# Decode attention: P as the stationary operand of PV, and an identity that stays loaded

## Chip, cores, metric

One core of one Trainium2 chip. The metric is the device time of one execution, in microseconds. The kernel before takes 1312.33 us (median of three runs, 1312.21 to 1312.5).

## The reference, cut

One decoded token, 32 heads of width 128, each with its own cache of 32,768 keys and values, in parallel with a SwiGLU block on the same normalised input. All inputs are bf16.

```python
xn = layernorm(x)                                        # (1, 1, 640)
q  = (xn @ wq).reshape(1, 1, 32, 128)
s  = einsum("bhqd,bhkd->bhqk", q, k_cache) * 128 ** -0.5  # 32768 scores per head
o  = einsum("bhqk,bhkd->bhqd", softmax(s), v_cache)
out = x + o.reshape(1, 1, 4096) @ wo + (silu(xn @ w_gate) * (xn @ w_up)) @ w_down
```

K and V are 537 MB of the 554 MB that have to be read. Nothing of them is used twice.

## The kernel before, the parts that matter

Keys lie as 128 partitions times 256. A unit of load is a chunk of 128 keys a partition: 4 MiB, 32 KiB a partition. A ring of six such slots holds K and V chunks by turns; the sync engine issues every load, in order, each as soon as its slot is free. VectorE multiplies K by q in place, TensorE (PE) adds up the 128 products of a key in 16 groups of eight, with an identity as the stationary operand, and VectorE sums the eight that are left. ScalarE makes P from the scores of a head. PV goes one key column at a time.

```python
units = [("wq",), ("ffn",)]
for h in range(H):
    for c in range(NCH):                      # NCH = 2 chunks a head
        units.append(("k", h, c))
        if h >= 1:
            units.append(("v", h - 1, c))
units += [("wo",)]
units += [("v", H - 1, c) for c in range(NCH)]
# ... slots by position modulo 6 ...

def scores(k):                                # TensorE, 2 halves a chunk
    ...
    for g in range(DH // G):                  # 16 matmuls of 512 columns a half
        mm = t.matmul(ob, lhsT=ident[:, :], rhs=kv[:, i * HF:(i + 1) * HF, g * G:(g + 1) * G],
                      start=(g == 0), stop=(g == DH // G - 1))
    mm.then_inc(s_qk, 1)                      # frees the K slot after the second half

def pv_ops(h, c):                             # TensorE, 128 times a chunk
    ...
    mm = t.matmul(O[h % 2], lhsT=ring[:, s, j * DH:(j + 1) * DH],     # V: 128 x 128, stationary
                  rhs=P[:, h % PR, jj:jj + 1], start=(jj == 0), stop=(jj == NJ - 1))
    ...
    mm.then_inc(s_pv, 1)                      # frees the V slot

# sync engine: a V load waits until PV of the chunk that lay there is done
e.dma_start(ring[:, s, :], kv_src(A_v_cache, h, c * CH, CH)).then_inc(s_slot[s], 16)
```

Every matmul here is two instructions in the program, a weight load and the matmul. The kernel is fully unrolled: 22,786 instructions in the trace, 21,692 of them weight loads and matmuls.

## Time and profile before

| | before |
|---|---|
| median time, us | 1312.33 |
| TensorE matmul busy / weight load busy / VectorE busy, us | 852.6 / 492.8 / 682.5 |
| mean granted TensorE clock | 0.731 |
| loads of K, V, weights: MB, share of 16 DMA engines' span | 554.0, 98.8% |
| instruction fetch (queue 8): packets, MB, share | 85, 1.39, 0.4% |

In the profile's lines PE stands for TensorE's matmuls, PEld for its weight loads, DVE for VectorE, ACT for ScalarE, POOL for GpSimd, SPq for the sync engine that issues the loads; L235 is line 235 of that run's kernel, and x is a count. From the page of the kernel before: the busy line of the engines, then three rows of 40 slices of the span (the clock in tenths, the DMA engines' busy share in tenths, the rate), and two of the DMA queues (packets, MB, share of 16 engines' span).

```profile
span 1310.3 us, 22786 instructions
...
PE 852.6 (65%) x10846; PEld 492.8 (38%) x10846; DVE 682.5 (52%) x405; ACT 31.6 (2%) x108; POOL 1.1 (0%) x8
...
PEclk9677776776776766776776776776776766776775
DMA  9999999999999999999999999999999999999987
GB/s 394 431 430 429 430 431 429 430 430 431 431 431 430 429 429 431 430 430 430 429 431 430 430 431 430 429 432 431 430 429 429 430 431 431 430 431 430 430 352 295
...
q1 hardware_dynamic: 23920, 554.00, 98.8%
q8 instruction: 85, 1.39, 0.4%
```

The reader is to see a DMA row of nines, and 429 to 432 GB/s from the second to the 38th slice, while TensorE's clock goes up and down between 0.6 and 0.8. So the stream of loads is the limit and the engines follow it. The two last slices are lower: there lie the loads of wo, in packets of 1,280 bytes, and the end. And there is a small queue 8, of the kind "instruction", with 1.39 MB and 0.4% of the 16 DMA engines' time: in this table the instructions themselves come over the DMA engines too.

Groups of instructions and DMA issues of the page of before (count, busy us, mean ns of one, idle before; for the issues, KB each and median us from issue to landing):

```profile
L235 PE MATMUL ps<-ring,ident 128*128 128x512 bf16 x2048 | 585.8, 457 | 417.9 <-DVE ring L439 417.9
...
L257 PEld LDWEIGHTS ps<-P,ring 128*128 128x128 bf16 x8192 | 219.1, 97 | 20.4 <-issue 10.5
L257 PE MATMUL ps<-P,ring 128*128 128x1 bf16 x8192 | 221.3, 163 | 5.7 <-DMA ring<-in_A_v_cache_dram 5.2
...
ring<-in_A_k_cache_dram SPq DMA_DIRECT2D x64, 4096.0 KB, 45.1
ring<-in_A_v_cache_dram SPq DMA_DIRECT2D x63, 4096.0 KB, 51.5
```

A K load takes 45.1 us from issue to landing where 4 MiB at 430 GB/s are 9.75 us: about 35 us of loads are always queued ahead of it. The sync engine's own waits for slots (us in total, times, longest):

```profile
SPq L174 <- PE ps L235: 934.8, 60, 18.8
SPq L184 <- PE ps L257: 184.4, 59, 3.3
```

Timeline of before near 617 us (start, duration, engine, line, operation, count), one score chunk and the PV after it:

```profile
617.16 0.13 PEld L235 LDWEIGHTS ps<-ring,ident 128*128 128x128 bf16 x2 [6.76 <-DVE ring L439]
...
619.28 0.15 PEld L235 LDWEIGHTS ps<-ring,ident 128*128 128x128 bf16 x1 [0.28 <-issue]
619.71 0.15 PEld L235 LDWEIGHTS ps<-ring,ident 128*128 128x128 bf16 x1 [0.28 <-issue]
...
626.42 3.44 PEld L257 LDWEIGHTS ps<-P,ring 128*128 128x128 bf16 x128
626.53 3.41 PE L257 MATMUL ps<-P,ring 128*128 128x1 bf16 x128
```

In the first stretch the weight loads, and so the matmuls, are 427 ns apart (619.28 to 619.71, clock 0.5). PV of a whole V chunk, 128 weight loads and 128 matmuls, is done in 3.4 us.

### The profile page before, as it was taken

What the parts mean: (1) busy time and instruction counts of PE and PEld (TensorE: products, weight loads), DVE (VectorE), ACT (ScalarE), POOL (GpSimd) and SP (SyncE); (2) the same over time, 40 slices, a digit from 0 to 9 for tenths busy, and PEclk for the clock granted to TensorE, in tenths of its full rate; (3) what the DMA queues carried; (4) which work ended last, traced back from release to release, by engine and by line L of the source; (5) the groups of instructions that cost most, each with busy time, mean ns of one, the idle gap of its engine ahead of it and who ended that gap; (6) DMA issues with size and microseconds to landing.
All of it is one profiled execution on the core that took longest, in us unless ns stands there. A gap on an engine that the chain in (4) does not pass through costs nothing.

```text
span 1310.3 us, 22786 instructions
## 1 busy us (share of the span) xinstructions
PE 852.6 (65%) x10846; PEld 492.8 (38%) x10846; DVE 682.5 (52%) x405; ACT 31.6 (2%) x108; POOL 1.1 (0%) x8
## 2 busy tenths in 40 slices
PE   3777675675675676675675675675675676675675
PEld 1534342343343333342433342333433333343434
DVE  0566456455456455456455456455456455456450
ACT  2000000000000000000000000000000000000000
POOL 0000000000000000000000000000000000000000
PEclk9677776776776766776776776776776766776775
DMA  9999999999999999999999999999999999999987
GB/s 394 431 430 429 430 431 429 430 430 431 431 431 430 429 429 431 430 430 430 429 431 430 430 431 430 429 432 431 430 429 429 430 431 431 430 431 430 430 352 295
DMA packets 24011, 555.45 MB, mean 424 GB/s; under 512 B 2480, under 2 KB 6640, under 8 KB 6896
## 3 DMA queue, kind: packets, MB, share of 16 engines
q1 hardware_dynamic: 23920, 554.00, 98.8%
q8 instruction: 85, 1.39, 0.4%
q14 instruction: 6, 0.05, 0.0%
HBM read 553.99 MB, written 0.00 MB: 423 GB/s over the span
## 4 chain that ended last, share of the span: by engine, by line
DMA 73%; PE 17%; DVE 8%; SPq 1%; issue 0%; DVEq 0%
DMA ring<-in_A_k_cache_dram 71%; PE ps L235 17%; DVE ring L439 8%; DMA ring<-in_A_v_cache_dram 2%; SPq L184 0%; SPq L179 0%; SPq L189 0%; DVE sc L447 0%; PE ps L257 0%; SPq L191 0%; DVEq L435 0%; SPq L188 0%; DVE pmax L454 0%; SPq L187 0%; SPq L170 0%
## 5 line engine op out<-in xcount | busy, mean ns | idle before, releaser
L235 PE MATMUL ps<-ring,ident 128*128 128x512 bf16 x2048 | 585.8, 457 | 417.9 <-DVE ring L439 417.9
L439 DVE TENSOR_TENSOR ring<-ring,qb 128x8192 bf16<-128x8192 bf16 x128 | 560.7, 4422 | 206.4 <-DMA ring<-in_A_k_cache_dram 206.4
L235 PEld LDWEIGHTS ps<-ring,ident 128*128 128x128 bf16 x2048 | 228.6, 114 | 749.4 <-DVE ring L439 423.6
L447 DVE TENSOR_REDUCE sc<-ps 128x64 f32<-128x512 f32 x128 | 88.5, 692 | 270.1 <-PE ps L235 270.1
L257 PEld LDWEIGHTS ps<-P,ring 128*128 128x128 bf16 x8192 | 219.1, 97 | 20.4 <-issue 10.5
L257 PE MATMUL ps<-P,ring 128*128 128x1 bf16 x8192 | 221.3, 163 | 5.7 <-DMA ring<-in_A_v_cache_dram 5.2
L368 ACT ACTIVATE P<-sc,negb 128x256 bf16<-128x256 f32 x32 | 16.2, 507 | 1214.6 <-DVE negb L462 1214.6
L462 DVE TENSOR_SCALAR negb<-ps 128x1 f32<-128x1 f32 x32 | 5.1, 158 | 56.8 <-PE ps L286 56.8
L457 DVE TENSOR_REDUCE m<-ps 1x1 f32<-1x128 f32 x32 | 8.9, 279 | 23.6 <-PE ps L280 23.6
L219 PE MATMUL ps<-ring,xnb 128*128 128x512 bf16 x40 | 11.0, 444 | 11.7 <-DMA ring<-in_A_wq_dram 11.7
L411 DVE TENSOR_SCALAR sg<-sg 128x13 f32<-128x13 f32 (+1 forms) x2 | 0.2, 157 | 34.9 <-ACT sg L351 34.9
L286 PE MATMUL ps<-m,ones 1*128 1x1 f32 x64 | 14.5, 293 | 0.4 <-DVE m L457 0.4
L454 DVE TENSOR_REDUCE pmax<-sc 128x1 f32<-128x256 f32 x32 | 13.4, 420 | 1.1
L274 PEld LDWEIGHTS ps<-rsum,ones 128*128 128x128 f32 x64 | 12.3, 194 | 4.5
L280 PE MATMUL ps<-identf,pmax 128*1 128x128 f32 x64 | 12.1, 271 | 1.2 <-DVE pmax L454 1.2
L286 PEld LDWEIGHTS ps<-m,ones 1*128 1x128 f32 x64 | 11.8, 228 | 1.2 <-DVE m L457 0.7
L427 DVE RECIPROCAL rzb<-ps 128x1 f32<-128x1 f32 x32 | 5.1, 158 | 13.6 <-PE ps L274 13.6
L295 PE MATMUL ps<-xn,ring 128*128 128x1 bf16 (+1 forms) x140 | 8.7, 198 | 5.0 <-DMA ring<-in_B_w_down_dram 5.0
L311 PE MATMUL ps<-ocol,ring 128*128 128x1 bf16 x160 | 6.7, 178 | 7.3 <-DMA ring<-in_A_wo_dram 6.9
L219 PEld LDWEIGHTS ps<-ring,xnb 128*128 128x128 bf16 x40 | 4.3, 110 | 17.9 <-issue 14.8
L295 PEld LDWEIGHTS ps<-xn,ring 128*128 128x128 bf16 (+1 forms) x140 | 8.6, 161 | 5.5 <-issue 5.4
L311 PEld LDWEIGHTS ps<-ocol,ring 128*128 128x128 bf16 x160 | 6.6, 131 | 7.4 <-DMA ring<-in_A_wo_dram 7.0
(40 smaller groups left out, 46.5 us busy)
## 6 DMA issues: line engine op xcount, KB each, us to landing
ring<-in_A_k_cache_dram SPq DMA_DIRECT2D x64, 4096.0 KB, 45.1
ring<-in_A_v_cache_dram SPq DMA_DIRECT2D x63, 4096.0 KB, 51.5
ring<-in_A_wq_dram SPq DMA_DIRECT2D x1, 5120.0 KB, 15.3
ring<-in_A_wo_dram SPq DMA_DIRECT2D x1, 5120.0 KB, 45.3
ring<-in_B_w_gate_dram SPq DMA_DIRECT2D x1, 2160.0 KB, 20.0
ring<-in_B_w_up_dram SPq DMA_DIRECT2D x1, 2160.0 KB, 24.7
ring<-in_B_w_down_dram SPq DMA_DIRECT2D x1, 2080.0 KB, 28.6
ring<-in_A_v_cache_dram SPq DMA_DIRECT2D x1, 2048.0 KB, 21.3
```

The lines of the kernel that those rows point to most:

```text
L219: mm = t.matmul(bank[b], lhsT=xnb[:, c, :], rhs=wq_v[:, c, b * 512:(b + 1) * 512], start=(c == 0), stop=(c == NCD - 1))
L235: mm = t.matmul(ob, lhsT=ident[:, :], rhs=kv[:, i * HF:(i + 1) * HF, g * G:(g + 1) * G], start=(g == 0), stop=(g == DH // G - 1))
L257: mm = t.matmul(O[h % 2], lhsT=ring[:, s, j * DH:(j + 1) * DH], rhs=P[:, h % PR, jj:jj + 1], start=(jj == 0), stop=(jj == NJ - 1))
L274: t.matmul(misc[:, 129:130], lhsT=ones[:, :], rhs=rsum[:, h % SR:h % SR + 1], start=True, stop=True).then_inc(s_z, 1)
L280: t.matmul(misc[0:1, 0:128], lhsT=pmax[:, h % SR:h % SR + 1], rhs=identf[:, :], start=True, stop=True).then_inc(s_t, 1)
L286: t.matmul(misc[:, 128:129], lhsT=ones[0:1, :], rhs=m1[0:1, h % SR:h % SR + 1], start=True, stop=True).then_inc(s_b, 1)
L295: mm = t.matmul(misc[0:n, off + j:off + j + 1], lhsT=hidden(w, c, j), rhs=xn[:, c:c + 1], start=(c == 0), stop=(c == NCD - 1))
L311: mm = t.matmul(acc[:, c:c + 1], lhsT=wo_v[:, h, :, c], rhs=ocol[:, h:h + 1], start=False, stop=(h == H - 1), skip_group_check=True)
L368: a.activation(out=P[:, h % PR, :], in_=sc[:, h % SCR, :], func=ACTF.Exp, bias=negb[:, h % SR:h % SR + 1], scale=c_scale, accum_out=rsum[: ...
L439: v.tensor_tensor(out=kh, in0=kh, in1=q[:, None, :].to_broadcast([128, HF, DH]), op=ALU.mult).then_inc(s_mul, 1)
L447: v.tensor_reduce(out=sc[:, h % SCR, j:j + HF], in_=bank[n % NBK].rearrange("p (j e) -> p j e", e=G), axis=AX.X, op=ALU.add).then_inc(s_re ...
L454: v.tensor_reduce(out=pmax[:, h % SR:h % SR + 1], in_=sc[:, h % SCR, :], axis=AX.X, op=ALU.max).then_inc(s_max, 1)
```

## The change

Intent: let P be stationary, four columns of it, and let 512 columns of V (four keys of a partition) move. That makes 32 matmuls of PV a chunk in place of 128. The result is a 4 x 512 block of which four 1 x 128 blocks on a diagonal are wanted; they are evicted once a head, scaled, and folded to one column by four small matmuls. Further, 15 of 16 score matmuls no longer reload the identity. To make room, a score buffer goes and a broadcast copy of xn moves into the ring. The result of the SwiGLU block is added to x early, since the fold uses its bank of PSUM (the memory in which this kernel's matmuls leave their sums). The last head keeps the old form. The diff, cut to its core:

```diff
-    SCR = 3
+    SCR = 2
+    W = 512 // DH
@@ scores
+                def again(out, lhsT, rhs, stop):
+                    return t.add_instruction(mybir.InstMatmult(
+                        start_tensor_calc=False, stop_tensor_calc=stop, ...
+                        ldweights=False, ...))
...
-                            mm = t.matmul(ob, lhsT=ident[:, :], rhs=kv[...], start=(g == 0), stop=...)
+                            src = kv[:, i * HF:(i + 1) * HF, g * G:(g + 1) * G]
+                            if g == 0:
+                                t.matmul(ob, lhsT=ident[:, :], rhs=src, start=True, stop=False)
+                            else:
+                                mm = again(ob, ident[:, :], src, g == DH // G - 1)
@@ pv_ops
+                            if h == H - 1:
+                                ...                                        # as before
+                            else:
+                                mm = t.matmul(O[h % 2], lhsT=P[:, h % PR, jj:jj + W],
+                                              rhs=ring[:, s, j * DH:(j + W) * DH], start=(jj == 0),
+                                              stop=(jj + W == NJ))
+                                j += W
@@ new
+                def fold(h):
+                    t.wait_ge(s_o4, h + 1)
+                    ...
+                    for m in range(W):
+                        mm = t.matmul(fold_ps, lhsT=o4[:, m * DH:(m + 1) * DH], rhs=identf[0:W, m:m + 1],
+                                      start=(m == 0), stop=(m == W - 1))
+                    mm.then_inc(s_fold, 1)
@@ vector
+                v.wait_ge(s_fpd, 1)
+                v.tensor_tensor(out=xf[:, :], in0=xf[:, :], in1=acc, op=ALU.add).then_inc(s_fx, 1)
... (buffers, semaphores, ScalarE's second eviction left out)
```

## The prediction

> **What bounds it now.** The DMA stream. The page's DMA table gives queue 1 98.8% of 16 engines' span for 554.0 MB; the 40 slices show 429 to 432 GB/s from the second to the 38th. In windows of 180 to 250 us between 50 and 1230 us the DMA share is 1.00 and the rate 430 GB/s. [...] 554.0 MB at 430 GB/s is 1288 us; the rest of 1312 is a slow first load, small-packet weights of the output projection, and 4.6 us after the last V landing (1305.7).
>
> PE (TensorE) is 65% busy, VectorE 52%. The chain of waits is 73% DMA; its 17% PE and 8% VectorE lie between a K landing and the reissue of its slot: latency inside the ring. The DMA issues show 45 us (K) and 51 us (V) from issue to landing, while 4 MiB at 430 GB/s takes 9.75 us: about 35 us of transfers stand queued ahead of each load.
>
> **What the change does, per pair of a K and a V chunk (19.5 us of DMA).**
> - PV: now 128 weight loads with one-column matmuls, 3.4 us (timeline near 626 us, 27 ns each). After: 32 matmuls of 512 moving columns. Score matmuls of that width are spaced 427 ns at clock 0.5 and about 213 ns at 1.00 in the same timeline; so PV takes an estimated 6.9 us warm, at most 13.7 us cold: slower by 3.5 to 10 us.
> - Scores: 30 of 32 identity loads go, but they already overlap; the matmuls are spaced by their 512 columns. Worth nearly nothing.
> - Fold and second eviction: under 2 us a head, not waited for by any load.
> - PE need: about 14 us warm to 18 us half cold, against 19.5. Fully cold it would be 27 us, but the timeline shows the clock going from 0.5 to 1.00 after some 4.5 us of matmuls.
> - V's slot comes free 3.5 to 10 us later; some 31 us of slack from the ring of six absorbs it. The lost score buffer costs nothing.
> - Start: VectorE waits for the down projection (3 us at 43 us); the K slots have over 25 us of slack.
> - End: the last head keeps the old form.
> - Instructions: about 21,700 PE instructions become about 8,400. Queue 8 (instruction fetch) carried 1.39 MB; some 0.85 MB goes: at 430 GB/s an estimated 2 us, the only gain on the critical path.
>
> **Prediction.** 1310.5 us, 1307 to 1315 eight times in ten. Faster by over 2%: 0.01; within 2%: 0.94; slower by over 2%: 0.05.
>
> **What would show it.** DMA share 1.00 and 430 GB/s in the same slices; queue 8 at about 0.55 MB. PE busy up from 853 to 1000-1200 us, the growth in PV's matmuls (221 to 430-600 us); granted clock up from 0.73 to 0.8-0.95. Weight-load busy down from 493 to 50-100 us. VectorE's busy time unchanged, its main wait still K landing. The sync engine's waits for a V slot end a few us later with no hole in the DMA row; V's issue to landing falls to 38-50 us.
>
> **What would make it wrong.** The clock staying near 0.5 with PE full: then the DMA row shows holes and the time exceeds 1400 us. Or extra moving reads slowing the DMA writes (below 425 GB/s in the middle). Or a semaphore of the fold delaying scores by over 30 us a head. Or instruction fetch sharing DMA time otherwise than by bytes: a few us either way.

(The forecast is the 1312.3 us of before less an estimated 2 us of fetch, put at 1310.5. Its "under 2 us a head" had no measurement yet; in the changed kernel the fold's matmuls of a head took 1.03 us and the second eviction 0.68 us, in the timeline near 608 us.)

## The result

1302.61 us (median of four runs, 1302.17 to 1302.89) against 1312.27 us (four runs of the kernel before): 9.7 us less. The ratio is 0.9927, 95% interval 0.991 to 0.9944. The result is correct.

From the page of the changed kernel, the same lines:

```profile
span 1300.1 us, 9523 instructions
...
PE 1056.5 (81%) x5142; PEld 261.4 (20%) x3222; DVE 678.1 (52%) x406; ACT 50.8 (4%) x139; POOL 1.1 (0%) x8
...
PEclk9689899988989989889988899988899998989996
DMA  9999999999999999999999999999999999999997
GB/s 396 428 426 435 433 429 428 433 435 427 435 429 434 427 433 431 432 429 433 432 432 425 434 433 431 431 430 436 428 430 432 433 430 429 433 432 430 429 407 315
...
q1 hardware_dynamic: 23920, 554.00, 99.5%
q8 instruction: 33, 0.54, 0.2%
```

The rate in the middle slices is about as it was, 425 to 436 GB/s, and the DMA row is as full. TensorE is busier (1056.5 against 852.6 us) at a higher clock (0.908), and the trace has 9,523 instructions in all, 8,364 of them TensorE's weight loads and matmuls (21,692 before). Queue 8 fell from 85 packets to 33. The span is 10 us shorter all the same.

Groups and issues of the changed kernel:

```profile
L233 PE MATMUL ps<-ring,ident 128*128 128x512 bf16 x1920 | 508.6, 425 | 0.0
L279 PE MATMUL ps<-ring,P 128*4 128x512 bf16 x1984 | 443.3, 379 | 0.0
L279 PEld LDWEIGHTS ps<-ring,P 128*4 128x4 bf16 x1984 | 163.4, 85 | 346.7 <-issue 109.4
...
ring<-in_A_k_cache_dram SPq DMA_DIRECT2D x64, 4096.0 KB, 44.5
ring<-in_A_v_cache_dram SPq DMA_DIRECT2D x63, 4096.0 KB, 47.1
```

The sync engine's waits for slots in the changed kernel:

```profile
SPq L180 <- PE ps L233: 711.1, 60, 16.3
SPq L190 <- PE ps L279: 402.4, 59, 6.9
```

Timeline of the changed kernel, PV of a chunk and a group of score matmuls:

```profile
621.72 7.07 PE L279 MATMUL ps<-ring,P 128*4 128x512 bf16 x32
...
631.99 3.40 PE L233 MATMUL ps<-ring,ident 128*128 128x512 bf16 x15
```

PV of a chunk takes 7.07 us in place of 3.4. The sync engine waits for a V slot 6.8 us each time (402.4 / 59) in place of 3.1 (184.4 / 59). Neither has made a hole in the DMA row.

### Where the 10 us are

The traces have 16 landing times for each load (2,224 for 139 loads in either kernel), read here as one for each of the 16 DMA engines, when its share has landed; the trace does not name the engine. On this reading their spread says how far the DMA engines have drifted apart. No view of `prof` prints these times; they are read from the packed trace. For the last K chunk (head 31, second chunk), counted from the span's start, and for the last piece of V:

```
                         before              after
K of head 31, first DMA engine  1245.2 us    1245.4 us
K of head 31, last DMA engine   1261.4 us    1251.9 us
lag of the 16, before: 0 .2 .2 .5 .8 .9 1.2 4.0 | 15.5 15.5 15.6 15.6 15.6 15.9 16.0 16.2
lag of the 16, after:  0 .0 .2 .5 .9 1.3 1.4 4.1 | 4.7 4.8 5.0 6.2 6.2 6.4 6.4 6.6
last piece of V, last engine    1305.7 us    1295.4 us
```

The fastest DMA engine is at the same place in both kernels after 1245 us. Half of the engines lag in both, and the lag of the last went from 16.2 to 6.6 us. That difference, 9.6 us, is nearly all of the 10.2 us between the spans of these two profiled executions (the medians differ by 9.7). The lag grows through the whole run (before: 1.9 us at 91 us, 8.2 at 574 us, 13.0 at 967 us), in steps of about 1.5 us with hardly a change between them.

The packets of queue 8 fit this. There are 85 before and 33 after, all of 16 KiB, one for 256 TensorE instructions (21,692 / 256 = 84.7, and 8,364 / 256 = 32.7). Their durations repeat in a cycle of eight (in ns, before, the packets from 158.9 us on: 1018 1080 1069 1060 1100 1099 1094 1018; from 286.7 us: 1016 1073 1069 1068 1098 1100 1085 1024; from 410.9 us: 1026 1073 1067 1060 1099 1107 1085 1018), as if eight DMA engines served them by turns. 52 packets fewer are 6.5 fewer for each of eight engines, and 9.7 / 6.5 = 1.49 us for each.

The steps of the lag say the same without the gain. In the changed kernel the last engine's lag is 1.6 to 2.0 us until 342 us, 3.1 to 3.6 from 352 to 682, 4.6 to 5.0 from 692 to 1032, and 6.2 to 6.6 from 1041 to 1255 (times are those of a load's first landing); the 9th, 17th and 25th packet of queue 8 start at 348, 694 and 1040 us. In the kernel before, the lag rises ten times, each time within the three loads that land after an eighth packet starts (the 8th at 149 us, the 16th at 273, and so to the 80th at 1250). Between steps it stays, although PV and the weight loads go on in every chunk. So the delay comes with the fetch packets, one in eight of which falls on the engine that is last; three steps from 2.0 to 6.6 us are 1.5 us each.

So the fetch was not hidden here, where the DMA engines are the limit: it fell on the loads, 9.7 us for 52 packets.

The end of the span shows it from the other side. Stretches of 4 us near the end of before (busy time and count of PE, PEld, DVE, ACT, POOL; then clock, DMA share, GB/s):

```profile
1268.00:1272.00 4.00, 4.00 (x14) 1.60 (x13) 2.46 (x2) 0.00 (x0) 0.00 (x0) 0.70 0.64 245
1272.00:1276.00 4.00, 4.00 (x53) 2.30 (x51) 1.20 (x3) 0.00 (x0) 0.00 (x0) 1.00 0.54 201
1276.00:1280.00 4.00, 3.12 (x101) 2.77 (x97) 0.85 (x3) 0.65 (x3) 0.00 (x0) 1.00 0.65 231
1280.00:1284.00 4.00, 0.00 (x0) 0.00 (x0) 0.00 (x0) 0.10 (x1) 0.00 (x0) 0.58 1.01 374
```

Between 1268 and 1280 us the DMA engines are only 54 to 65% busy: the fast ones have run out of work while the slow ones are still at the projection weights (wo landed from eight engines between 1269.2 and 1273.0 us, and from the other eight between 1283.8 and 1286.0). The same stretches of the changed kernel:

```profile
1268.00:1272.00 4.00, 4.00 (x23) 1.71 (x20) 0.28 (x1) 0.00 (x0) 0.00 (x0) 1.00 1.10 383
1272.00:1276.00 4.00, 2.01 (x19) 1.84 (x19) 0.16 (x1) 1.54 (x5) 0.00 (x0) 0.88 1.06 419
1276.00:1280.00 4.00, 4.00 (x102) 4.00 (x103) 0.00 (x0) 0.00 (x0) 0.00 (x0) 0.50 0.97 418
1280.00:1284.00 4.00, 2.72 (x60) 2.63 (x58) 0.17 (x1) 0.00 (x0) 0.00 (x0) 0.50 1.03 438
```

No such hole: the lag is smaller. (The sync engine needs 24.0 us before, and 22.75 us after, for the one issue of V of head 31 behind the small packets of wo; that the fast engines could not be given their share meanwhile is an inference.)

### The profile page after: what moved, and what is told of

The parts are those of the page before. It is cut to its first block, busy times and chain, and to the rows that moved or that the text cites. A ratio compares the mean times of both kernels' runs of the same rounds, so it can differ in the third digit from the quotient of the medians.

```text
span 1300.1 us, 9523 instructions
## 1 busy us (share of the span) xinstructions
PE 1056.5 (81%) x5142; PEld 261.4 (20%) x3222; DVE 678.1 (52%) x406; ACT 50.8 (4%) x139; POOL 1.1 (0%) x8
## 4 chain that ended last, share of the span: by engine, by line
DMA 51%; PE 32%; DVE 16%; SPq 1%; issue 0%; DVEq 0%; ACT 0%
DMA ring<-in_A_k_cache_dram 47%; PE ps L233 18%; DVE ring L488 15%; PE ps L279 10%; DMA ring<-in_B_w_down_dram 2%; DMA ring<-in_A_v_cache_dram 2%; PE ps L250 2%; PE ps L330 1%; PE ps L321 0%; SPq L190 0%; PE ps L315 0%; PE ps L338 0%; SPq L185 0%; SPq L195 0%; DVE sc L496 0%
## 5 line engine op out<-in xcount | busy, mean ns | idle before, releaser
L488 DVE TENSOR_TENSOR ring<-ring,qb 128x8192 bf16<-128x8192 bf16 x128 | 560.6, 4421 | 117.0 <-DMA ring<-in_A_k_cache_dram 117.0
L233 PE MATMUL ps<-ring,ident 128*128 128x512 bf16 x1920 | 508.6, 425 | 0.0
L279 PE MATMUL ps<-ring,P 128*4 128x512 bf16 x1984 | 443.3, 379 | 0.0
L279 PEld LDWEIGHTS ps<-ring,P 128*4 128x4 bf16 x1984 | 163.4, 85 | 346.7 <-issue 109.4
L250 PE MATMUL ps<-ring,ident 128*128 128x512 bf16 x128 | 55.7, 435 | 209.0 <-DVE ring L488 209.0
L496 DVE TENSOR_REDUCE sc<-ps 128x64 f32<-128x512 f32 x128 | 88.3, 690 | 243.8 <-PE ps L233 243.8
L250 PEld LDWEIGHTS ps<-ring,ident 128*128 128x128 bf16 x128 | 12.6, 98 | 518.8 <-DVE ring L488 421.5
L300 PE MATMUL ps<-identf,o 4*128 4x1 f32 x248 | 31.8, 245 | 0.9 <-ACT o L395 0.9
L300 PEld LDWEIGHTS ps<-identf,o 4*128 4x128 f32 x248 | 30.0, 187 | 0.9 <-ACT o L395 0.9
L225 PE MATMUL ps<-ring 128*128 128x512 bf16 x40 | 11.5, 461 | 11.9 <-DMA ring<-in_A_wq_dram 11.9
L395 ACT ACTIVATE o<-ps,rzb 4x512 f32<-4x512 f32 x31 | 21.0, 677 | 0.0
L275 PE MATMUL ps<-P,ring 128*128 128x1 bf16 x256 | 7.6, 165 | 5.7 <-DMA ring<-in_A_v_cache_dram 5.1
## 6 DMA issues: line engine op xcount, KB each, us to landing
ring<-in_A_v_cache_dram SPq DMA_DIRECT2D x63, 4096.0 KB, 47.1
```

Source lines behind the costliest of these rows:

```text
L233: return t.add_instruction(mybir.InstMatmult(start_tensor_calc=False, stop_tensor_calc=stop, tile_size=(128, 128), tile_position=(0, 0), l ...
L250: t.matmul(ob, lhsT=ident[:, :], rhs=src, start=True, stop=False)
L279: mm = t.matmul(O[h % 2], lhsT=P[:, h % PR, jj:jj + W], rhs=ring[:, s, j * DH:(j + W) * DH], start=(jj == 0), stop=(jj + W == NJ))
L300: mm = t.matmul(fold_ps, lhsT=o4[:, m * DH:(m + 1) * DH], rhs=identf[0:W, m:m + 1], start=(m == 0), stop=(m == W - 1))
L395: a.activation(out=o4[:, :], in_=O[h % 2], func=ACTF.Copy, scale=rzb[0:W, h % SR:h % SR + 1]).then_inc(s_o4, 1)
L488: v.tensor_tensor(out=kh, in0=kh, in1=q[:, None, :].to_broadcast([128, HF, DH]), op=ALU.mult).then_inc(s_mul, 1)
```

## Experiments

Theory A: instruction fetch for TensorE falls on eight of the sixteen DMA engines by turns and holds each up some 1.5 us a packet; since the loads are queued deeply, the delays add up, and the end comes with the most delayed engine. Rivals: B, weight loads read on-chip memory and slow the DMA writes; C, the new form of PV or the higher clock makes the gain; D, the prediction's own view, fetched bytes shared evenly by all engines.

| run | built on | packets of queue 8 | median us | before | difference | median lag of the slower 8 / lag of the last (K of head 31), us |
|---|---|---|---|---|---|---|
| before | | 85 | 1312.27 | | | 15.6 / 16.2 |
| after | | 33 | 1302.61 | 1312.27 | -9.7 | 6.2 / 6.6 |
| e1_ident_only | before | 78 | 1310.25 | 1311.88 | -1.6 | 14.4 / 16.7 |
| e2_pv_only | after | 41 | 1303.60 | 1311.88 | -8.3 | 7.8 / 8.2 |
| e4_fill_pool | after | 33, and 39 more of queue 14 | 1320.64 | 1311.88 | +8.8 | 6.4 / 26.1 |
| e11_before_pv_twice_half | before | 117 | 1317.89 | 1312.05 | +5.8 | 21.7 / 21.9 |
| e3_fill_pe | after | 53 | 1449.27 | 1311.88 | +137.4 | 0.4 / 0.6, holes in the stream |
| e5_before_fill_pe | before | 104 | 1363.42 | 1311.76 | +51.7 | 1.1 / 2.3, holes |
| e10_before_pv_twice | before | 147 | 1373.16 | 1312.05 | +61.1 | 0.3 / 2.0, holes |
| e6_after_shift_1mb | after | | 1330.79 | 1311.76 | +19.0 | see below |
| e7_before_shift_2mb | before | | 1350.39 | 1311.76 | +38.6 | see below |

### The two parts of the change alone

The identity part alone, on the kernel before:

```diff
-                            mm = t.matmul(ob, lhsT=ident[:, :], rhs=kv[...], start=(g == 0), stop=(g == DH // G - 1))
+                            src = kv[:, i * HF:(i + 1) * HF, g * G:(g + 1) * G]
+                            if g == 0:
+                                t.matmul(ob, lhsT=ident[:, :], rhs=src, start=True, stop=False)
+                            else:
+                                mm = again(ob, ident[:, :], src, g == DH // G - 1)
```

> The kernel before, with only the second part of the change: 1,920 identity loads fewer, PV as before. Theory A (instruction fetch: queue 8's 16 KiB packets fall on 8 of the 16 DMA engines in turn, each holds its engine up some 1.5 us, and the last load ends with the most delayed engine): 7.5 packets fewer of 85, so about 1.4 us less, 1310.9 us against 1312.3; last-engine lag at K of head 31 from 16.2 to about 14.8 us. Theory B (weight loads read SBUF and slow the DMA writes, in proportion to their busy time: about 216 of the 231 us that the change removed go here): about 9 us less, 1303 us. Theory C (the gain is PV's form or the higher clock): no change, 1312.3. Theory D (my prediction: fetched bytes shared evenly by all engines): 0.3 us less.

Measured: 1310.25 us (five runs, 1309.98 to 1310.83) against 1311.88, 1.6 us less (ratio 0.9989, interval 0.9976 to 1.0001, so by itself at the edge of what can be told from nothing, though the slowest of its five runs lies below the fastest of the nine of before, 1311.36). From its page:

```profile
PE 858.7 (66%) x10846; PEld 277.4 (21%) x8926; DVE 682.4 (52%) x405; ACT 31.6 (2%) x108; POOL 1.1 (0%) x8
...
q8 instruction: 78, 1.28, 0.4%
```

It removes 215 us of weight-load time (492.8 to 277.4 us), nearly all that the change removes, and yet not 9 us come of it: B falls, as it was put. The median of the eight slower engines' lags went from 15.6 to 14.4 us as A has it, but the last engine's did not (16.7, a miss: one engine stood 2 us behind the other seven there).

The PV part alone is the changed kernel with the same lines turned back:

```diff
-                            if g == 0:
-                                t.matmul(ob, lhsT=ident[:, :], rhs=src, start=True, stop=False)
-                            else:
-                                mm = again(ob, ident[:, :], src, g == DH // G - 1)
+                            mm = t.matmul(ob, lhsT=ident[:, :], rhs=kv[...], start=(g == 0), stop=(g == DH // G - 1))
```

> The changed kernel with the identity reloaded for every score matmul, so the PV part of the change alone: about 10,300 PE instructions, 41 packets of queue 8. Theory A: 8 packets more than after, one per fetching engine, so about 1.5 us more, 1304.1 us; lag at K of head 31 about 8 us. Theory B: about 9 us more than after, 1311. Theory C: as after, 1302.6. Theory D: 0.3 us more than after.

Measured: 1303.60 us (five runs), 8.3 us less than before (ratio 0.9938, interval 0.9925 to 0.995). Its queue 8:

```profile
q8 instruction: 41, 0.67, 0.2%
```

Its 41 packets are 44 fewer than before, 5.5 for each engine, and 8.3 / 5.5 = 1.51 us. The last lag is 8.2 us, expected 8. The parts add up: 1.6 and 8.3 against 9.7 for both. This run by itself doesn't tell A from C, since most of the gain is in the PV part and both expect that.

### More instructions, nothing else: on GpSimd

```diff
+                for _ in range(156 * NK):          # GpSimd, after its two constants
+                    g.wait_ge(s_const, 4)          # long satisfied
```

> The changed kernel with the same 4,992 extra instructions on the idle GpSimd instead. Which DMA engines carry that engine's fetch is not known. Theory A: if they are the same 8, as in the run with the fill on TensorE, about 3.7 us more than after; if they are the 8 others, no change, since those have over 4 us to spare at the end; if one engine carries all 19.5 packets, up to 25 us more; all of it within the first part of the span, but the lag should stay to the end. Theories B and C: as after, 1302.6. Theory D: 0.75 us more.

Measured: 1320.64 us (five runs; ratio to before 1.0068, interval 1.0055 to 1.0081), 18.0 us more than the changed kernel's 1302.61. (It was run at another time.) That is A's third case, one engine that carries all; A had left three outcomes open here, so the run tests the rivals harder than A. From its page:

```profile
span 1318.4 us, 14516 instructions
...
GB/s 391 428 430 433 430 432 431 429 428 430 432 430 431 430 433 430 431 430 432 430 431 433 432 431 430 430 432 430 431 433 432 431 431 430 430 433 430 430 242 262
...
q8 instruction: 33, 0.54, 0.2%
q14 instruction: 46, 0.38, 0.1%
```

GpSimd's instructions come over queue 14, which carries 0.3 MB more than in the changed kernel, in packets of 8 KiB, 39 more. The middle slices are as before, and the last two are low (242 and 262 GB/s). The 16 landings of K of head 31 say why: 15 engines are within 6.7 us, as in the changed kernel, and one is 26.1 us behind. The lag was there after 591 us (25.8 us) and stayed, since the fill was over by about 450 us. So 0.06% of the bytes cost 1.4% of the time, through instructions that have nothing to do with TensorE, its weight loads or its clock: B and C have no place for this cost, and D (0.75 us) is far off. That C adds nothing to the gain itself is not shown by this run but by the lag, which holds 9.6 us of it. The run shows A's core, that the most delayed DMA engine sets the end.

### More instructions on TensorE, and two that went wrong

```diff
 # e3_fill_pe, on the changed kernel
                     scores(k)
+                    for _ in range(156):
+                        t.wait_ge(s_const, 4)      # two to an instruction: 78
 # e5_before_fill_pe, on the kernel before
+                    if k:
+                        for _ in range(156):
+                            t.wait_ge(s_const, 4)
                     scores(k)
```

> The changed kernel with 78 extra TensorE sequencer instructions (waits that are already satisfied) after each of the 64 score chunks: 4,992 instructions, 19.5 packets of queue 8, no added work on any array or engine. Theory A: 2.4 packets more on each fetching engine, 3.7 us more than after, 1306.3 us, lag at K of head 31 from 6.6 to about 10.2 us. Theories B and C: as after, 1302.6. Theory D (bytes shared evenly, 0.32 MB at 430 GB/s): 0.75 us more. If the extra instructions hold TensorE up so that it cannot keep pace, DMA holes would show in the middle slices and the time would be higher than 1307; then the run says little.

> The kernel before with 78 satisfied-wait instructions on TensorE ahead of each score chunk but the first (4,914 in all, 19.2 packets of queue 8, 2.4 for each fetching engine); the fill on the changed kernel took 3.1 us a chunk and stood between two engines that wait on each other, here TensorE has 6 to 7 us free per pair and the fill stands after PV. Theory A (fetch on 8 of 16 DMA engines in turn, some 1.5 us each, the last load ends with the most delayed engine): 3.6 us more than before, about 1315.5 us, lag at K of head 31 from 16.2 to about 20 us. Theory D (bytes shared evenly): 0.75 us more. Theories B (weight loads) and C (form of PV, clock): as before. A DMA hole in the middle slices would spoil the reading again.

Measured: 1449.27 us and 1363.42 us. Rates of the fill on the changed kernel:

```profile
GB/s 401 433 424 434 433 429 406 378 372 409 398 389 367 370 399 408 392 373 383 384 372 409 404 380 377 363 404 410 392 368 388 379 378 407 392 391 381 363 308 117
```

and of the fill on the kernel before:

```profile
GB/s 395 431 431 430 430 428 429 429 429 430 429 430 421 424 408 420 424 404 414 418 408 409 411 398 416 411 412 419 414 410 415 412 406 410 403 415 415 412 316 172
```

In both the rate falls in the middle slices, which both expectations named as the sign that the run says little. The fill cost more than thought: the trace records its instructions 106 ns apart in both kernels, so that a chunk's fill takes TensorE's sequencer 8.5 to 8.8 us (medians), and TensorE could not keep pace. The 3.1 us in the second expectation were only the part of it in which TensorE's matmuls stood still; during the rest, matmuls issued earlier were still running. Two things can be read from them. Where the loads are not queued deeply (a K load lands 14.7 and 15.1 us after its issue, 45.1 in the kernel before), the lag is gone (0.6 and 2.3 us), so an engine that is behind catches up in a hole. And the changed kernel has less room than a 31 us slack sounds: that slack is for one late release, not for a longer period. Some 8.5 us more of TensorE's instruction stream in every pair broke it, and in e10 (below) so did 3.4 us of double PV on the kernel before.

A cleaner way is instructions that TensorE runs through fast: issue PV's matmuls of the kernel before twice, in the even heads, the copy into an unused column.

```diff
+            TWIN = [ps8[:, 6, 16:17], ps8[:, 6, 17:18]]
...
+                            if h < H - 1 and h % 2 == 0:        # the full one: h < H - 1
+                                t.matmul(TWIN[h % 2], lhsT=ring[:, s, j * DH:(j + 1) * DH],
+                                         rhs=P[:, h % PR, jj:jj + 1], start=True, stop=True, skip_group_check=True)
                             mm = t.matmul(O[h % 2], lhsT=ring[:, s, j * DH:(j + 1) * DH], ...)
```

> The same for the 16 even heads of 0 to 30: 8,192 instructions, 32 packets more. Theory A: 4 more per fetching engine, 6.0 us more than before, 1317.8 us, lag about 22 us. Theory D: 1.2 us more. Theory C: none.

> As the refused e8, the copy now in an unused column of PSUM bank 6, which no other engine reads meanwhile. The kernel before with every PV matmul of heads 0 to 30 issued twice: 7,936 weight loads and as many one-column matmuls more, 15,872 instructions, 62 packets of queue 8 on top of 85. TensorE's own work rises by 3.4 us a pair, from about 12.8 to 16.2 of 19.5 us, so it should still keep pace. Theory A (fetch packets on 8 of 16 DMA engines in turn, some 1.5 us each): 7.75 more per fetching engine, 11.7 us more than before, 1323.5 us; lag at K of head 31 from 16.2 to about 28 us. Theory D (bytes shared evenly, 1.02 MB at 430 GB/s): 2.4 us more, 1314.3. Theory C (clock, form of PV): none.

The half measured 1317.89 us (five runs, 1317.81 to 1318.13), 5.8 us more than before (ratio 1.0046, interval 1.0032 to 1.0059); expected 1317.8. From its page:

```profile
span 1316.0 us, 30978 instructions
...
GB/s 392 430 430 432 428 428 432 429 429 429 429 431 431 428 429 432 429 429 429 429 430 429 430 429 430 430 430 429 430 428 430 428 430 430 432 428 429 430 315 296
...
q8 instruction: 117, 1.92, 0.6%
```

The middle is at 428 to 432 GB/s, queue 8 has 32 packets more, the last lag is 21.9 us, expected 22. D (1.2 us) and C (none) fall. 5.8 us for 4 packets an engine are 1.45 us each. The added instructions are no empty ones, though: 4,096 weight loads of V and as many matmuls. A narrower B, that it is PV's weight loads (which e1 leaves alone) that slow half of the DMA engines, was not tested by a run of its own. The steps of the lag at every eighth packet, with PV going on evenly between them, and the GpSimd fill speak against it. The result of this run is wrong (relative error 0.998); the copy shares a PSUM bank with the running output sum, and whether that is the reason was not tested. The values steer no timing in this kernel.

The full one has the same wrong result and missed: 1373.16 us instead of 1323.5. Its rates:

```profile
GB/s 392 433 429 432 427 431 426 429 428 430 429 431 430 429 402 418 420 425 417 404 389 412 417 410 415 404 399 414 403 373 423 413 414 401 429 394 400 389 324 140
```

From the 15th slice on the stream has holes: TensorE and VectorE, which wait on each other in every chunk, no longer keep up when every head has the double PV. Up to 280 us, with the stream still full, its last lag was 6.6 us where before had 3.5 us at the same load: the lag grew faster, as A has it.

### Moving bytes from the slow engines to the fast ones

```diff
+                    elif u == ("v", H - 1, 0):
+                        src = kv_src(A_v_cache, H - 1, 0, CH)
+                        e.dma_start(ring[0:LOW, s, :], src[0:LOW, :]).then_inc(s_slot[s], 16)
+                        for p in range(LOW, 128, 8):
+                            e.dma_start(ring[p:p + 8, s, :], src[p:p + 8, :]).then_inc(s_low, 16)
```

with LOW = 96 on the changed kernel and 64 on the kernel before.

> The changed kernel with one load cut differently: of V of the last head, first chunk, 96 partitions go as before and 32 partitions as four loads of 8 partitions each. [...] Theory A: the end moves by about 2.4 us; earlier (1300.2 us)[...], later (1305)[...]. No instruction of TensorE changes. Any theory that puts the gain in TensorE's work, its clock or its weight loads: no change (1302.6), or a slight loss from five issues in place of one.

> The kernel before with the same cut, 64 partitions on all engines and 64 partitions as eight loads of 8 partitions[...]. TensorE's program is that of before but for one wait. Theory A: 4.8 us earlier than before, about 1307 us,[...] or 4.8 us later, about 1317[...]. Theories B, C and D: as before, 1311.9.

(The 2.4 and 4.8 us are estimates: 64 and 128 KiB more on each of eight engines, at a sixteenth of 430 GB/s. Whether theory A has the end earlier or later hung on which eight engines they are.)

Measured: 1330.79 and 1350.39 us, far slower than any theory had it. Stretches near the end of the second (columns as before; the first stretch is ahead of the cut load, the others are in it):

```profile
1250.00:1255.00 5.00, 5.00 (x25) 2.25 (x23) 1.38 (x2) 0.00 (x0) 0.00 (x0) 0.99 0.96 408
1300.00:1305.00 5.00, 0.00 (x0) 0.00 (x0) 0.00 (x0) 0.00 (x0) 0.00 (x0) 0.50 0.88 105
1310.00:1315.00 5.00, 0.00 (x0) 0.00 (x0) 0.00 (x0) 0.00 (x0) 0.00 (x0) 0.50 1.01 111
```

While the small loads are under way the core moves 105 to 111 GB/s in place of 408, with the DMA engines still 88 to 101% busy. Why was not tested. As to the number of engines, the eight small loads of the second run have 72 recorded semaphore updates, one near each issue and eight landings for each load, which fits eight engines a load; which eight the trace doesn't show. The cut load was a bad probe, it tells nothing between the theories, and no version that beats both kernels came of it.

## Why the prediction was wrong, point by point

- **What bounds the kernel: right.** The stream of loads did, before and after; the middle rate moved by less than 1%. But the end of the stream is set by its most delayed DMA engine, which the prediction did not ask for.
- **PV slower, by 3.5 to 10 us a chunk: right**, 7.07 against 3.4 us. The ring took it: no hole in the DMA row, and the waits for a V slot are 3.7 us longer each.
- **The wrong step:** "Queue 8 (instruction fetch) carried 1.39 MB; some 0.85 MB goes: at 430 GB/s an estimated 2 us, the only gain on the critical path." That fetch traffic is the gain was right, and so were its bytes (0.85 MB went, 1.39 to 0.54). What failed is the way it turns bytes into time, evenly over all sixteen engines at the full rate: the term of 2 us measured 9.7 us. Two factors were missed. The packets fall on eight engines, not sixteen, which doubles the share of each. And a packet holds its engine up 1.49 us, where a data packet of the same 16 KiB takes 0.61 us in this trace: 2.44 times as much. 2.0 us x 2 x 2.44 = 9.8 us. (The 1.49 us is worked back from the gain, so this product is book-keeping and no test. Figures that don't come from it are the steps of the lag, about 1.5 us, and 1.45 us of the run with the half double PV, for which 6.0 us had been written down beforehand and 5.8 came.) The table of queues gave a warning that was not used: 85 packets took 0.4% of 16 engines' span, while they are 0.25% of the bytes. The line on "instruction fetch sharing DMA time otherwise than by bytes" named the risk, and put it at a few us; the range, 1307 to 1315, did not hold it.
- **Identity reloads worth nearly nothing: right for TensorE** (all matmuls busy 858.7 us with the identity kept, 852.6 before), and yet some 1.6 us in time, at the edge of the noise, with 1,920 instructions fewer.
- **Granted clock 0.8 to 0.95, PE busy 1000 to 1200, V landing 38 to 50 us, queue 8 about 0.55 MB: right** (0.908, 1056.5, 47.1, 0.54).
- **Weight-load busy 50 to 100 us: wrong**, 261.4. A load of four columns takes 85 ns, hardly less than one of 128 (97 on the page of before, 98 on that of the changed kernel). In a row they overlap: PV's 128 loads of 128 columns in the kernel before took 3.44 us together, 27 ns each. No hole in the DMA row came of it.
- **VectorE's main wait is K landing: wrong** for both kernels. It is the wait for the score matmuls (270.1 us before, 243.8 after); K landing was 206.4 and is 117.0.
- **Slack of 31 us: right for one late release**, and no measure of how much longer a period may get: 3.4 us more PV in every chunk, or 8.5 us of fill, broke the stream.

What stays open: why a fetch packet that lasts 1.07 us delays its engine by 1.49 (and one of GpSimd's 8 KiB, which lasts 0.31 us, by some 0.6), and which eight engines serve TensorE's fetch; the trace does not name the engine of a packet, so "eight by turns" rests on the cycle of durations, the eight lagging engines, and the size and the moments of the steps. A run that adds TensorE instructions alone, with no work on the array and no holes, was tried twice and did not succeed.

## What to carry to other kernels

Where the DMA engines bound a kernel, as here, instructions are traffic too: 52 fetch packets fewer were worth 9.7 us, their bytes over the total rate only 2. Count the packets of the fetch queue, ask which DMA engines carry them, and size the cost by the most delayed engine, not by bytes over the total rate. The spread of a load's sixteen landing times shows this drift (16.2 us before, 6.6 after), which busy shares and rates in slices hide (430 GB/s in the middle of both). Fewer instructions can pay even where they make the engine that runs them slower: here TensorE's matmuls were busy 1056.5 us in place of 852.6, and the time fell by 9.7.
